# Banded attention into a gated conv feed-forward: another order table, with part of the output stores issued by GpSimd

## The chip, the cores and the metric

One core of a Trainium2 chip. The metric is the device time of one execution in microseconds; of several runs the median is given. PE is the TensorE matrix engine, DVE VectorE, ACT ScalarE, POOL GpSimd, and SP the queue engine that issues most transfers here.

## The reference

Inputs q, k, v are [8, 8, 576, 64] float32: 8 batches, 8 heads, 576 positions, head size 64. The feed-forward has w_in [512, 1024], conv_w [3, 1024] and w_out [1024, 512].

```python
scores = (q @ k.transpose) / 8
scores = where(|i - j| <= 32, scores, -1e9)
attn = softmax(scores) @ v
x = attn, heads side by side              # [8, 576, 512]
h = maximum(x @ w_in, 0)                  # [8, 576, 1024]
conv = sum over 3 taps k of conv_w[k] * h shifted by k - 1 positions
out = (h * sigmoid(conv)) @ w_out         # [8, 576, 512]
```

## The kernel before

The kernel first builds a list of operations (`Work.op`), each with a name, what it reads and writes, and the slots of buffers it takes. Nothing is issued then. Afterwards `Work.emit` walks through a text, `ORDER`, written out in full: each token is an operation's number, the letter of the engine that issues it (P for PE, V for DVE, S for ACT, G for POOL, D for a transfer on SP's queue) and the buffer indices it takes. `1F` lets PE do one idle matmul. All engines keep this order (`keep_in_program_order`), so the text fixes, for every engine, what runs after what, and which engine does each operation that several could do.

Attention, for each batch b: `load q/k b i` brings four heads of q or k into a slot of the pool `st` (0.59 MB each), `cast` makes bf16 from it into `qkb`, `tr` transposes on PE into PSUM, `ev` evicts into `qkT`. `sc` computes the scores of a half (x) of a head group in three PSUM banks, with only the 128 keys that a block of 64 queries can see; `exp` on ACT writes them to `attn`, `mask` multiplies by 0 and 1 (for batch 0, `sca` adds a large negative matrix on PE before the scores, and there is no mask). `load v b c` and `cast v b c` bring a 128-row piece of v with a border of 32 into `ve`; `vo hi` and `vo lo` copy its halves into `vo`, shifted by 64 rows. `av` multiplies, `rec` takes the reciprocal of the row sums, `mul` writes `xn`. A turn then makes `xT`: `xt` on PE and `ex` (kind e), or a transposing transfer `xd` (kind d), by the table `TURNS`.

The feed-forward works on chunks c = 0 to 11 of 384 positions, three for each pair of batches, and on eight blocks m of 128 of the 1024 columns. `ph` is four matmuls with `w_in_sb` (385 columns or so), `relu` writes `hT` (pools hT0, hT1, hT2 by the chunk's place in the pair). The convolution's three taps are shared out by a letter for each block in `CONV`: 3, 2 and 1 are the number of taps that PE does by diagonal matrices `diag_w` (`pc`), the rest on DVE (`tap`); q lets POOL multiply two taps (`cp`) and add them (`cs`) and DVE the third; r one tap on POOL, two on DVE; s two on POOL, one on PE, with a `sum` on DVE. `tanh` on ACT, `gate` on DVE to `gT`, then `py` multiplies by `w_out_sb`, `y` evicts 128 rows to a slot of the pool `y`, and `store c i` writes them out (0.26 MB). Chunk 1 is done in two halves (`SPLIT`).

w_in comes in three transfers (`load w_in 0, 1, 2`: columns 0 to 255, 256 to 511, 512 to 1023) and is cast block by block; w_out in two. The number of buffers of each pool is in `BUFS`.

The letters of the engines mean, in the two helpers that matter here:

```python
loader = {"D": sync, "Q": scalar}
...
loader[e_].dma_start(out_rows[r0:r0 + 128, :], y_sb.ap)
```

Of the kernel before, what the change touches and what calls it, by code (L numbers as in the profile page):

```python
# [40 lines left out]
class Work:  # L41
# [45 lines left out]
BUFS = {'st': 3, 'qkb': 6, 'qkT': 3, 'attn': 2, 'rec': 6, 'xn': 2, 'hT0': 7, 'hT1': 9, 'hT2': 9, 'cp': 6, 'gT': 3, 'y': 6}  # L87
TURNS = ('eeeee', 'eeede', 'eeeed', 'ddddd', 'ddddd', 'ddddd', 'ddddd', 'ddddd')
MASKS = ('aa', 'mm', 'mm', 'mm', 'mm', 'mm', 'mm', 'mm')
CONV = (  # L90
    'r2333q33',
    '221223s321s2213r',
    'r3q3332s',
    'r333s3q3',
    '22q33q33',
    'q32sqq2q',
    '33qq2rqq',
    '2q3q3qrr',
    'qqrqqq33',
    '32qrqqqr',  # L100
    'rqq2qq3q',
    '2r22qqrq',
)
ORDER = """
11D0 12D 13D1 14D 16D 18D 15D 22S0 0V 19D 20G1 41P010 23V 21G 42P 45P23 43S 46P 48S 44V 47V 17D 124D2 24S2 28G 125D
50P4560 52S 51S 25V 61P031 26V3 27S 1P1 2V 62P 64S 3V 126D0 65P25 66P 67S 33G 29V 35G 68V 56P413 63S 135D1 59S 53S
58S 70P2501 76P361 30G 36G 71S 31S 79S 73S 57S 4V 34V 77S 81P20 90P1 72S 78S 84P0 93P4 85V0 37V 91V1 82V2 38G 99P3
86V 92V 94V3 32S 100V4 40V 117P5 102P6 83V 103V5 104V 39G 8G 136D 140D 2F 130G 111P0 112V0 113V 108P1 109V1 110V
127G 128G 95S 88P2 118V2 97P6 89V 129G 101S 106P0 98V 115P1 131G 1F 141D 139D 137D2 132G 1F 107S 116S 250P4 294P2
138D 133V 119V 134V 240D0 251S00 10V 360P3 262G0 142D 145V4 144S5 295S1 361V2 272P6 273S3 7V 149S 263V0 264V 338P1  # L110
1F 339V4 161P542 162S 164P23 368G12 275P6 276V 270S 271V 165V 369G 163S 370G 5G 382P7 292S 293V 166S 155V 6G 122P1
316P5 317V5 296P0 371V2 167P4631 314S 146G1 171S 383S6 170S 169S 123V 380S 315V 150G 241D1 404P5 179P370 405S0 180V
381V 995D 340P6 358S 154G 173P410 318P5 176S 181V 359V 147G0 9G 406P3 438P2 244V 992D2 182P17 148G 336S 424S 337V
439S01 384P6 183S 245V 425V 243G 177S 151G 482P5 483V1 402S 526P2 504P1 403V 184S 185P3050 441P6 172V 158V 994D 153G
527S2 175S 178V 529P7 530V 159V 187S 188S 570P2 592P4 460P3 143D 461V3 593S4 548P0 546S 547V 996D 487P3 249G 189S
571S5 191P475 195S 242G 426P2 190V 194S 463P5 430P7 585G34 549V6 246V 197P01 488V 248S 464V 156G 442V 505S7 206P1
157G 247G 193S 196V 215P4 458S 427P 459V 507P6 480S 481V 428S0 200P5 216V5 431P 1001G2 198V0 508V 990D0 489V 586G
207V1 199S 991D 218P2 217V 209P0 201V3 997D 594P4 524S 208V 152G 998D 502S 503V 434P1 432S1 550P3 160G 525V 202V
219V4 210V2 211V 233P7 224P6 234V0 227P5 228V5 435P 225V1 235V 587G 204P0 226V 213P7 220S 222P6 568S 229V 993D 612S
436S2 205V 214S 1030P251 613V 238P1 658P0 724P7 1003G 223S 1032S 614P4 659S3 1031V 999G3 230D 1000G5 702P6 1091D1  # L120
1092D 615S1 569V 725V2 729P5 617P0 703S4 239S 673G50 768P2 769S5 730V 1012P432 1093D0 705P7 618V 1006G 731V 1004V
634S 1013S 1015P61 706V 744S 635V 1014S 1016S 636P2 745V 1005V 637V0 680P4 1007G 588P0 1094D 589V 1002G4 681V6 722S
723V 746P3 1033P65 747S1 1034V 1096D 1017S 802P2 1018P4731 641P6 676P1 1011V 674G 1035S 642V 590S 780G2 803S82 675G
677V 824P5 846P2 643V 1020S 1022S 790P4 678S 1021S 656S 825V2 1100G1 1101S0 591V 679V 657V 683P3 781V7 684V 1024P501
1027S 791P 1023V 847S0 814G1 748P6 1026S 792V3 1028S 766S 700S 1113P020 1114S 1116P54 782V 1009G 1115V 701V 815V1
1118S 767V 1095D 1097D 1102G2 1131P022 1132S 1133S 826P3 844S 1117V 854G43 855G 1029V 1036P4600 1038S 1040S 868P2
788S 890P5 794P4 1039S 437D 1758D2 856G 816V 857V0 789V 891S3 866S 429D 1103G3 1042P675 1106G 869V1 1010V 870P2 795P
1098D 867V 845V 822S 823V 1104V 1134P03 1045S 1099D 1105V 793D 1044S 1046S 1047V 1008G 1048P10 1057P7 1066P5 1049V3
1058V2 1756D1 796S4 934P6 1135S 912P4 1067V0 888S 1050V 1041G 1762D 1084P0 1069P1 889V 1075P2 1136S 956P3 935S7
892P6 1110G 1085V1 1076V4 1757D 1070V5 913S4 1071V 1051P4 1086V 1078P1 1060P0 1079V3 1759D 1059S 798P7 1767G5 1760D  # L130
1107S 1077S 937P2 957V6 914P3 1068V 799P 1111G 433D 971G05 972G 973G 1061V5 910S 911V 1062S 1064P5 932S 1052V1 1053V
1108S 800S5 1080V 938V 954S 1065V 1761D 1055P6 1073P0 1082P4 933V 955V 978P7 1074S 1765G4 1778P151 1766G1 1119P3201
1083S 974P4 1056V 1192P6 1763D 1779S 1857D0 1236P1 1122S 1112V 1214P2 1780V 1123S 1121S 1125P503 975V 976S 1193V20
1127S 982P6 1258P5 977V 983P 1109G 1215V4 1216P4 1129S 1124V 1204G2 1859D1 1768G0 1128S 1237S3 1205V2 1206V 1771S
1137P3010 979P 984V2 1259S0 1769G 1130G 1212S 1861D 1213V 1143P652 1234S 1235V 1770V 1141S 1139S 1149P41 1158P1
1176P3 1140S 980V0 1167P0 1772G 1177V2 1324P7 1168V4 1147S 1142V 1346P2 1146S 1145S 1775G 1238P5 1260P6 1325S6
1280P7 1860D 1159V0 1178V 1148V 1179P3 981D 1764D 1150V5 1151V 1152P4 1160S 1256S 1278S 1169V 1185P1 1776G 1332G13
1279V 1170P0 1347S1 1281S5 1171V1 1161P6 1180V3 1162V2 1181V 1333G 1087D 1302P2 1172S 1186V5 1303S2 1781P73 1782S
986P0 1334G 1298P2 1348P7 1163V 797D 1153V0 1154V 1295G45 1796P640 1257V 1296G 1297G 1783S 1187V 1335V5 1299V 1304P3
987P 1866G2 1344S 1366S 1862D 1368P1 1858D 1798V 1345V 1300S 1879P452 1797S 1182D 1301V 1868G3 1367V 1784P6271 1322S  # L140
1323V 988S3 1788S 985D 1799P30 1870V 1787S 1773G 1369P 1376P7 1880V 1088D 1800S 1881S 1790P243 1801V 1774D 1370V1
1802P5010 1377P 1869V4 1871G 1164D 1786S 1794S 1793S 1777V 1789V 1792S 1795V 1378S0 1897P631 1806S 1863D 1867G1
1372P4 1814P20 1823P7 1832P1 1804S 1841P5 1373P 1824V4 1872V 1898S 1155D 1864D 1833V3 1805S 2526D 1380P6 1834S 1825V
1374V4 1842V1 1808P017 1446P4 1843V 1873S 2522D2 1812S 2524D1 1424P5 1381S01 1402P7 1383P6 1811S 1810S 1815V2
1882P10 1816V 1173D 1512P2 1188D 1189D 1403S1 1405P7 2523D 1425V2 2529D 1899S 1807G 1813V 1817P5 1835P3 2525D 1447S3
1384V 1400S 1826P4 1865D 1883V 1406V 1468P1 1827V0 1836V5 1884S 1432G02 2531G5 1513S4 1490P0 1534P2 1828V 1448P4
1401V 1379D 1469V5 1470P6 1837S 1844P1 1422S 1433G 1875G 1818V3 1850P3 1434G 1535S6 1491V7 1829D 1423V 1819S 1466S
1467V 1900P20 2533G2 1488S 1901S 1845V4 1846V 1536P7 1568P5 1435V4 1569S52 1554S 1489V 1902S 1498G35 1851V1 1656P2
1444S 1514P1 1590P5 1612P6 1375D 2535G 1555V 2528D 1499G 1576G14 989D 1852V 1445V 1591S0 1500G 1885P0730 1887S
1634P4 801D 1577G 1613V2 1615P5 1657S8 1847D 1501V0 1889S 1616V 1592P6 1874G 1532S 1560P2 2532G0 1556P3 1533V 1510S  # L150
1838D 1511V 1578G 2534V3 1888S 1878D 1820D 1635S1 1890V 2537S 1876D 1891P107 1632S 1633V 1610S 1664G20 1611V 1894S
1557P 1561P 1903P4561 2527D 1579V0 1893S 1678P1 1853D 1895S 1562S2 1722P7 1896V 1558V0 1907S 1909P236 1588S 1589V
1905S 1906S 1915P01 1924P4 1679V3 1908V 1877G 1933P5 2536V 1934V2 1649G53 1650G 1651G 1913S 1652P1 1564P6 1723S4
1911S 1958P7 1912S 2623D0 1665G 1565P 1980P2 1666G 1653V 1916V0 1654S 1686G41 1925V5 1926S 1935V 1667V3 1914V 1918P4
1700P5 1959S40 1936P7 1655V 1687G 1676S 1927P1 2530D 1917V 2624D 1730G30 1731G 1981S0 1982P0 1919V3 1677V 1559D
1688G 2625D2 2024P2 1920S 1689V3 2626D 1566S4 1942P4 1928V4 1945P6 1854D 1937V1 1929V 1938V 1930D 2025V3 1951P1
1943V5 1952V2 1701S7 2540G 1567D 2000S 2539S 1698S 2538G 2543V 1944S 2001V 1946V0 2632G1 2002P7 2003S6 1921D 2032G52
1703P2 1960P5 2629D 1732G 2562P400 1947V 2564S 2033G 2544P762 1953V 1699V 2545S 2546V 1733V0 1704V 2068P1 2069S5
2046P3 2010G14 2011G 1744P7 2034G 2112P6 1978S 2541D 2563S 2047S1 1720S 1979V 1563D 2035V1 1742S 2012G 2049P4 1721V
# [36 lines left out]
def kernel(  # L196
# [40 lines left out]
    gpsimd, sync = InOrder(nc.gpsimd), InOrder(nc.sync)  # L237
# [9 lines left out]
    qkb = pool("qkb", [128, RP, 2, 64], BF16)  # L247
    qkT = pool("qkT", [128, 4, W], BF16)
# [466 lines left out]
    def project(c, i):  # L715
# [19 lines left out]
        def emit_st(e_):  # L735
            r0 = c * CH + 128 * i
            loader[e_].dma_start(out_rows[r0:r0 + 128, :], y_sb.ap)
# [113 lines left out]
```

## Time and profile before

| | |
|---|---|
| runs | 240.04, 242.59, 241.75 us; median 241.75 |
| the profiled execution | 240.04 us, of which the span in the profile is 238.3 |
| busy in the span | PE 206.2, DVE 213.1, ACT 181.2, POOL 189.0 us |
| mean granted clock of PE | 0.98 |
| transfers | 46.75 MB, nearly all on SP's queue |
| chain that ended last | DVE 43%, PE 26%, "issue" 11%, POOL 8%, ACT 6% |

Each profiled instruction belongs to a group named by its engine, the operation and its tiles (all have one line, since a helper records them): `pf` is PSUM, `cp` POOL's products, `gT` the gated block. A group's line gives the number, the busy time and the mean ns of one, then the idle time of the engine before them with what released it. Ends overlap the start of the next instruction on PE, DVE and ACT, so durations of rows add up to more than busy time.

### The profile page before, as it was taken

How to read it: one execution, taken by the hardware profiler on the slowest of the kernel's cores; microseconds unless marked ns; L12 is line 12 of the kernel's file. 1: busy time of each engine (PE TensorE's matmuls, PEld its weight loads, DVE VectorE, ACT ScalarE, POOL GpSimd, SP SyncE). 2: the span in 40 equal slices, each digit the busy share in tenths (PEclk: the TensorE clock that was granted, in tenths of full speed). 3: DMA queues.
4: the chain of work that ended last, by engine and by line, in shares of the span. 5: the costliest groups of instructions: out<-in, count | busy, mean ns of one | idle time of the engine just before them, and what ended most of it. 6: DMA issues, size and time to landing. Idle time of an engine off the chain costs nothing.

```text
span 238.3 us, 7024 instructions
## 1 busy us (share of the span) xinstructions
PE 206.2 (87%) x2615; PEld 118.8 (50%) x2637; DVE 213.1 (89%) x473; ACT 181.2 (76%) x456; POOL 189.0 (79%) x256
## 2 busy tenths in 40 slices
PE   0868987899899998999998889899899879998972
PEld 0545646467555645555654555454555435544420
DVE  6729999899998999997789999998998998999991
ACT  2894797689999878788979788796889856735651
POOL 7068699878798888945999999889769496999920
PEclk9995999999999999999999999999999999999997
DMA  6999999967999957989999969720247503421034
GB/s 224 298 254 373 274 350 298 268 172 232 301 288 352 222 191 211 234 186 254 296 261 149 356 181 189 170 54 3 87 95 143 200 30 101 105 79 53 0 133 177
DMA packets 68166, 46.75 MB, mean 196 GB/s; under 512 B 52172, under 2 KB 53220, under 8 KB 68132
## 3 DMA queue, kind: packets, MB, share of 16 engines
q1 hardware_dynamic: 68096, 46.30, 72.6%
q8 instruction: 20, 0.33, 0.6%
q14 instruction: 14, 0.11, 0.2%
q10 hardware_dynamic: 36, 0.01, 0.0%
HBM read 32.52 MB, written 9.44 MB: 176 GB/s over the span
## 4 chain that ended last, share of the span: by engine, by line
DVE 43%; PE 26%; issue 11%; POOL 8%; ACT 6%; DMA 3%; SPq 2%; DVEq 0%; POOLq 0%; ACTq 0%
PE pf L234 26%; DVE pf L234 13%; DVE gT L234 11%; DVE attn L234 4%; POOL cp L234 4%; DMA vst<-in_v_dram 3%; DVE hT L234 3%; DVE qkT L234 3%; ACT pf L234 2%; DVE vo L234 2%; POOL vo L234 2%; SPq L234 2%; DVE xn L234 2%; DVE y L234 2%; ACT attn L234 1%
## 5 line engine op out<-in xcount | busy, mean ns | idle before, releaser
L234 PE MATMUL pf<-xT,w_in_sb 128*128 128x385 bf16 (+2 forms) x416 | 73.6, 316 | 2.2 <-DVE hT L234 0.8
L234 POOL TENSOR_SCALAR cp<-hT,conv_w_sb 128x384 f32<-128x384 bf16 (+1 forms) x89 | 61.7, 703 | 16.1 <-ACT hT L234 9.4
L234 PE MATMUL pf<-w_out_sb,gT 128*128 128x512 bf16 x266 | 68.7, 380 | 4.8 <-DVE gT L234 3.2
L234 ACT ACTIVATE pf<-pf 128x384 f32<-128x384 f32 (+1 forms) x104 | 47.1, 469 | 26.3 <-DVE pf L234 24.7
L234 DVE SCALAR_TENSOR_TENSOR gT<-pf,hT 128x384 bf16<-128x384 f32 (+1 forms) x104 | 51.1, 515 | 2.2 <-ACT pf L234 1.3
L234 PEld LDWEIGHTS <-w_in_sb 128*128 128x128 bf16 x416 | 38.5, 98 | 26.3 <-issue 2.8
L234 ACT ACTIVATE attn<-pf 128x512 bf16<-128x512 f32 (+1 forms) x96 | 42.4, 510 | 3.2 <-PE pf L234 2.3
L234 DVE SCALAR_TENSOR_TENSOR pf<-hT,conv_w_sb,cp 128x384 f32<-128x384 bf16 (+1 forms) x46 | 40.4, 881 | 2.3 <-issue 0.7
L234 PEld LDWEIGHTS <-gT 128*128 128x128 bf16 x288 | 26.1, 98 | 32.4 <-DVE gT L234 6.1
L234 POOL TENSOR_TENSOR cp<-cp,cp 128x384 f32<-128x384 f32 (+1 forms) x38 | 40.1, 1061 | 1.9
L234 ACT ACTIVATE hT<-pf 128x385 bf16<-128x385 f32 (+2 forms) x73 | 34.2, 487 | 5.5 <-PE pf L234 5.0
L234 PE MATMUL pf<-hT,diag_w 128*128 128x384 bf16 (+1 forms) x138 | 28.4, 311 | 2.1 <-DVE hT L234 1.5
L234 POOL TENSOR_SCALAR qkb<-st 128x1152 bf16<-128x1152 f32 (+2 forms) x24 | 28.2, 1179 | 0.6 <-DMA st<-in_q_dram 0.3
L234 ACT COPY qkT<-pf 128x576 bf16<-128x576 bf16 x44 | 27.1, 658 | 1.8 <-DVE xn L234 1.0
L234 ACT ACTIVATE xn<-pf,rec 128x64 bf16<-128x64 f32 x88 | 20.3, 328 | 5.9 <-DVE rec L234 5.7
L234 DVE TENSOR_TENSOR attn<-attn,mask 128x1152 bf16<-128x1152 bf16 x23 | 24.5, 1069 | 0.1
L234 PE MATMUL pf<-ident,qkb 64*128 64x64 bf16 x576 | 15.7, 196 | 9.1 <-POOL qkb L234 5.9
L234 DVE SCALAR_TENSOR_TENSOR pf<-hT,conv_w_sb,pf 128x384 f32<-128x384 bf16 (+1 forms) x39 | 20.7, 542 | 1.7 <-PE pf L234 1.2
L234 POOL TENSOR_SCALAR vo<-ve 64x520 bf16<-64x520 bf16 (+1 forms) x20 | 19.6, 980 | 2.6 <-PE pf L234 0.8
L234 PEld LDWEIGHTS <-qkT 64*128 64x128 bf16 x576 | 13.0, 98 | 15.2 <-issue 13.8
L234 DVE TENSOR_TENSOR xn<-pf,rec 128x256 bf16<-128x256 f32 x50 | 19.8, 412 | 0.5
L234 PE MATMUL pf<-qkT 64*128 64x64 bf16 x576 | 16.1, 195 | 4.4 <-DVE gT L234 2.1
(54 smaller groups left out, 238.4 us busy)
## 6 DMA issues: line engine op xcount, KB each, us to landing
st<-in_q_dram SPq DMA_DIRECT2D x16, 576.0 KB, 5.7
st<-in_k_dram SPq DMA_DIRECT2D x16, 576.0 KB, 6.6
out_dram<-y SPq DMA_DIRECT2D x36, 256.0 KB, 2.6
vst<-in_v_dram SPq DMA_DIRECT2D x24, 256.0 KB, 5.9
vst<-in_v_dram SPq DMA_DIRECT2D x16, 192.0 KB, 5.1
st<-in_moe_w_out_dram SPq DMA_DIRECT2D x2, 1024.0 KB, 10.1
vo<-ve SPq DMA_DIRECT2D x9, 130.0 KB, 3.3
st<-in_moe_w_in_dram SPq DMA_DIRECT2D x2, 512.0 KB, 6.0
```

Of the source, the lines that this page charges most:

```text
L234: return lambda *args, **kwargs: fixed(do(*args, **kwargs))
```

## The change

The order table is another one from end to end, and with it the numbers of buffers, the engine that each operation is given, and the taps' letters. In the code one line is changed: a store whose letter is G is issued by GpSimd.

```diff
-BUFS = {'st': 3, 'qkb': 6, 'qkT': 3, 'attn': 2, 'rec': 6, 'xn': 2, 'hT0': 7, 'hT1': 9, 'hT2': 9, 'cp': 6, 'gT': 3, 'y': 6}
-TURNS = ('eeeee', 'eeede', 'eeeed', 'ddddd', ...
+BUFS = {'st': 4, 'qkb': 5, 'qkT': 3, 'attn': 2, 'rec': 7, 'xn': 2, 'hT0': 5, 'hT1': 8, 'hT2': 7, 'cp': 6, 'gT': 3, 'y': 5}
+TURNS = ('eeeee', 'deeee', 'eeeed', 'ddddd', ...
-    'r2333q33',  '221223s321s2213r', 'r3q3332s', 'r333s3q3', '22q33q33', 'q32sqq2q', ...
+    '32r233q3',  'q2233r3q322q3321', 's33r3333', '2233r233', '32q32323', 'q2qs23qq', ...
-11D0 12D 13D1 14D 16D 18D 15D 22S0 0V 19D 20G1 41P010 23V 21G 42P 45P23 43S 46P 48S 44V 47V 17D 124D2 24S2 28G 125D
+0V 11D0 13D1 12D 15D 124D2 14D 16D 19D 22S0 20V1 21G 18D 41P010 23S 42P 45P23 46P 28S 47V 48V 135D3 43S 17D 24G2
...
-            loader[e_].dma_start(out_rows[r0:r0 + 128, :], y_sb.ap)
+            (gpsimd if e_ == "G" else loader[e_]).dma_start(out_rows[r0:r0 + 128, :], y_sb.ap)
```

What the two tables give to the engines, where they differ (number of operations, old to new):

| operation | engines |
|---|---|
| store | SP 36 to 21, POOL 0 to 15 |
| mask | DVE 23 to 19, POOL 5 to 9 |
| `cp` products, `cs` additions | POOL 89 to 78, 38 to 32 |
| units with 3, 2, 1 taps on PE | 30 to 36, 20 to 20, 8 to 5 |
| first taps from a `q` or `r` unit | DVE 46 to 43 |
| `ev` | ACT 44 to 40, DVE 20 to 24 |
| `mul` | ACT 22 to 18, DVE 50 to 54 |
| cast v | POOL 19 to 24, ACT 11 to 10, DVE 10 to 6 |
| cast q and k | POOL 24 to 26, ACT 6 to 4, DVE 6 to 6 |
| cast w_in | POOL 6 to 5, ACT 0 to 3, DVE 2 to 0 |
| `vo` (half copies) | POOL 20 to 16, DVE 11 to 16, SP 9 to 8 |
| relu | ACT 73 to 76, DVE 31 to 28 |

The first loads on SP's queue, in order (w_in by part):

```
old: q 0 0, k 0 0, q 0 1, k 0 1, v 0 1, v 0 3, v 0 0, v 0 4, v 0 2, w_in 0, w_in 1, w_in 2, q 1 0
new: q 0 0, q 0 1, k 0 0, v 0 0, w_in 0, k 0 1, v 0 1, v 0 4, v 0 3, q 1 0, v 0 2, w_in 2, w_in 1
```

## The prediction

> **What bounds the kernel now.** I read the busy times first, then busy time by stage, then the opening microseconds instruction by instruction.
>
> ```profile
> PE 206.2 (87%) x2615; PEld 118.8 (50%) x2637; DVE 213.1 (89%) x473; ACT 181.2 (76%) x456; POOL 189.0 (79%) x256
> ...
> 0.00:23.80 23.80, 14.02 (x250) 9.68 (x251) 15.31 (x56) 14.80 (x33) 13.75 (x57) 0.86 0.92 287
> 23.80:60.00 36.20, 32.60 (x488) 21.38 (x492) 33.98 (x88) 29.65 (x76) 30.60 (x44) 0.99 0.97 268
> 60.00:120.00 60.00, 56.59 (x858) 33.29 (x864) 55.25 (x129) 52.37 (x137) 48.92 (x47) 1.00 0.97 252
> 120.00:180.00 60.00, 54.45 (x658) 30.38 (x662) 57.02 (x111) 49.62 (x129) 54.17 (x61) 1.00 0.68 155
> 180.00:238.30 58.30, 48.57 (x367) 24.03 (x371) 51.58 (x93) 34.79 (x86) 41.51 (x50) 0.98 0.33 100
> ```
>
> The columns after the stretch are PE, PEld, DVE, ACT and POOL. From 23.8 us on, DVE is busy 197.8 of 214.5 us (92%) and PE 192.2 (90%), POOL next. No single wait ends that part. Before 23.8 us no engine reaches two thirds: the opening waits for transfers.
>
> ```profile
> 6.28 0.62 ACT L234 CAST qkb<-st 128x512 bf16<-128x512 f32 x1 [3.52 <-DMA st<-in_k_dram]
> ...
> 10.21 0.43 DVE L234 CAST qkb<-st 128x512 bf16<-128x512 f32 x1 [1.14 <-DMA st<-in_k_dram]
> ...
> 13.66 0.62 POOL L234 TENSOR_SCALAR ve<-vst 128x512 bf16<-128x512 f32 x1 [7.47 <-DMA vst<-in_v_dram]
> ...
> 15.78 0.62 POOL L234 TENSOR_SCALAR ve<-vst 128x512 bf16<-128x512 f32 x1
> ...
> 22.17 1.20 POOL L234 TENSOR_SCALAR w_in_sb<-st 128x512 bf16<-128x512 f32 x2 [0.22 <-DMA st<-in_moe_w_in_dram]
> ...
> 23.82 3.60 PE L234 MATMUL pf<-xT,w_in_sb 128*128 128x385 bf16 x20 [0.32 <-ACT xT L234]
> ```
>
> These are start, duration, instruction, and the wait before it. They give landings in queue order: the first k half at 6.28 us, the second at 10.21, the last of five v pieces just before 15.78, w_in at 22.17. The first feed-forward matmul starts at 23.82.
>
> **Part 1, the opening loads: +4.1 us.** The old order was q0, k0, q1, k1, five v pieces, then w_in. The new one is q0, q1, k0, v 0, w_in part 0, k1, v 1, v 4, v 3, batch 1's q0, v 2, and w_in parts 2 and 1. Pace from the rows above: a q or k half (0.59 MB) takes (10.21 - 4.88)/3 = 1.78 us, q0 having landed at 4.88; a v piece takes (15.78 - 10.21)/5 = 1.1; w_in (2.1 MB) takes 6.4, so its first quarter takes 1.6. That puts k0 at 8.4 us, k1 at 12.8 (2.6 late), v 2 at 19.0 (3.2 late), all of w_in at 23.8.
>
> The chain behind k1 in the new table: DVE casts it, but halfway comes `cast v 0 1`, which needs a piece landing at 13.95; the last cast ends at 14.9. After `conv_ev` and one `vo`, three evictions of 0.75 us stand on DVE before the scores: 17.7. Scores of the second head group to 19.2, six exponentials on ACT to 21.5 (old: 14.96 + 2.40 = 17.36). Then eight `av` at 0.45 us on PE: 25.1; DVE's reciprocal and four `mul` of 0.42 queued behind: 27.0; transpose 0.35, eviction 0.6. The first `ph` starts at 27.95 instead of 23.82. On POOL, `cast v 0 2` waits for v 2, with `vo hi 0 0 1`, `vo hi 0 1 2` and the first w_in cast queued behind it; they end by 22.7, inside that chain. A later `cast w_in 3` waits till 23.8, also covered. Low end of this term: 1.3 us, the 3.2 of v 2 less 1.9 that PE loses today in waits for `vo`. High end: 5, if those waits come back.
>
> **Part 2, work moved between engines.** I count each table and price by row:
>
> ```profile
> L234 DVE TENSOR_TENSOR attn<-attn,mask 128x1152 bf16<-128x1152 bf16 x23 | 24.5, 1069 | 0.1
> ...
> L234 POOL TENSOR_TENSOR attn<-attn,mask 128x1152 bf16<-128x1152 bf16 x5 | 12.4, 2482 | 8.4 <-ACT attn L234 8.4
> ```
>
> The last figure before the second bar is ns of one: a mask moved to POOL costs 2.48 for 1.07. Four are moved.
>
> DVE: masks -4.3, four first taps of `q` units (0.88 each, and fewer of them at half width) -3.7, v casts -4 x 0.58 = -2.3, three relus -1.4, two w_in casts, a diagonal and a y -2.2, q and k casts and sums -1.0; added: 4 `ev` +3.0, 4 `mul` +1.7, 5 `vo` +3.3, one more `r` unit +1.5. Total -5.4. The durations of all rows sum to 237.6 where the page has 213.1 busy, since ends overlap the next start, so this is worth -4.9.
>
> PE: six more three-tap units and three fewer one-tap units, 15 diagonal matmuls more: at 28.4 us for 138 it is +3.1, and as PE's rows sum to 243.3 for 206.2 busy, +2.7. ACT: -4.1, not at the limit. POOL: eleven products fewer (mostly at 0.71) -8.1, six additions (1.09) -7.0, masks +9.9, casts of q, k and v +6.1, `vo` -4.5, a diagonal more and a w_in cast less +0.6; net -3.0, without stores.
>
> **Part 3, 15 of 36 stores on POOL.** What they leave behind is not on the path: SP already stands idle waiting for results, and after the opening no engine shows a wait for a load.
>
> ```profile
> SPq L234 <- ACT y L234: 32.1, 8, 12.0
> ...
> L234 SPq DMA_DIRECT2D out_dram<-y x36: 332/438/3545, 61.6 to 234.4; - x36
> ```
>
> (The waits of SP's queue; then min, median and max ns of a store's issue.) So no gain from SP. POOL's own price isn't in this trace. From below: SP's median, 0.44 us, 6.6 for 15. From above: POOL's longest row, 2.48, 37 for 15. The only row of a compute engine's queue issuing a transfer is ACT's, 0.65 us; I take that, 9.8 us. Against total work it puts POOL at 195.8. Fourteen of the 15 stand 18 or more operations behind their `y` in the table, so POOL rarely waits for data; where it does, the products behind it are late next, then DVE's taps. At the very end two POOL stores (10 0 and 11 2) follow each other: +0.5 us, between 0 and 2.
>
> The Trainium skill (page "SBUF — State Buffer", sections "SBUF: two separate sides" and "A bandwidth-pool intuition that's wrong") speaks against this part: a transfer issued by GpSimd has its descriptors written through a port pair that certain DVE instructions lock, about 0.62 us alone and 3.1 beside a DVE copy. By those figures 15 stores would cost between 9.3 and 46 us of POOL, as an estimate; the low figure agrees with the 9.8 taken from the row and leaves the sum as it is, the high one would make POOL the bound. A row here that fits a shared port is the DVE tap that reads two SBUF operands, 882 ns, beside 614 where one comes from PSUM; no run here shows a store on POOL.
>
> **The body's sum.** Busy work after the first `ph`, old to new: DVE 202.0 to 195.2, PE 194.6 to 197.1, POOL 177.9 to 185.9. If only the largest total counts, 202.0 becomes 197.1: -4.9. But an engine can run ahead only as far as buffers allow, and the new table is uneven: cut into stretches of two chunks (from one chunk's first `ph` to that of the second after it), adding the busiest engine of each, it gives 206.4 old, 206.1 new; in stretches of one chunk 211.2 and 215.9, because POOL leads in several (its masks and casts come in lumps). gT has three buffers, hT fewer than before (5, 8, 7 for 7, 9, 9), so I take the two-chunk sum, -0.3, with -4.9 and +4.7 as ends.
>
> Sum: +4.1 - 0.3 + 0.5 = +4.3 us, a span of 242.6. The profiled execution took 240.04 for its span of 238.3, so 244.3; it was the fastest of three, and on the median of 241.75 it would be 246.0. I say 245.2, between the two.
>
> **Rivals.**
> (a) DVE's relief decides (faster). The place is 23.8 to 220 us, the price -4.9, and the opening costs only its low end 1.3, no tail: -3.6, about 237.3. For it: DVE is the busiest engine now, and `gT` and `hT` waits are the largest ones of PE. Against: PE gets 2.7 us more. It decides where the opening costs less than 2.4.
> (b) Both happen: +4.1 + 0.5 - 4.9 = -0.3, about 240.6: no change. For it: the totals are only two engines' averages apart; against: the one-chunk sums.
> (c) POOL becomes the bound. At 1.25 us a store (what SP's transposes take, 1.23) the one-chunk sum is 220.1, +8.9; with the opening and a tail of 1 it is +14, about 255; at 2.48 by two chunks, +7.1 and a tail of 2, +13. For it: POOL leads in the uneven stretches. Against: the old POOL shows 16 us of idle before products.
>
> **How the numbers follow.** Forecast 0.42, with its own range 242.5 to 250; (a) 0.24; (b) 0.19; (c) 0.15. A measurement of this kernel tells about 1% from no change, 239.3 to 244.2. Faster is (a), 0.24; the same is (b), 0.19; slower is the forecast and (c), 0.57. The range leaves out (a)'s lowest part and (c)'s highest: 236.8 to 253.
>
> **What would show it.** Opening: the first matmul from `xT` near 28 us, POOL's `ve` cast waiting till 19 us. Body: DVE busy near 208, PE 209, POOL 196 with stores of about 0.65 us. Tail: last y to the end some 0.5 us longer than today's 3.9. I am wrong if the first `ph` starts before 25.5 us, or if DVE's share rises with PE's in the body.

## The result and the profile after

The changed kernel takes 250.94 us (median of four runs, 250.09 to 252.0) where the kernel before takes 241.53 beside it: a ratio of 1.040, with an interval of 1.032 to 1.047. It is 9.4 us slower. I had said 245.2, 3.5 us more: the direction was right, the size was not. The profiled execution took 252.0 us for a span of 250.3.

Busy times of the changed kernel:

```profile
PE 208.9 (83%) x2627; PEld 121.2 (48%) x2652; DVE 219.9 (88%) x463; ACT 176.3 (70%) x440; POOL 190.7 (76%) x258
```

PE went from 206.2 to 208.9, as worked out. DVE was to fall to 208 and rose to 219.9, with ten instructions fewer. That line points at the step that failed.

The same work by stages, cut at the first feed-forward matmul and at the first relu of chunks 2, 4 and 8. First the changed kernel, then the kernel before with its own moments (columns PE, PEld, DVE, ACT, POOL, then the granted clock):

```profile
0.00:27.38 27.38, 14.55 (x251) 10.14 (x252) 16.60 (x57) 13.79 (x32) 13.51 (x53) 1.00 1.03 289
27.38:66.50 39.12, 33.83 (x488) 22.68 (x491) 36.14 (x82) 28.15 (x74) 32.86 (x47) 0.91 0.85 244
66.50:124.30 57.80, 49.18 (x752) 28.08 (x760) 52.08 (x101) 43.53 (x113) 44.44 (x42) 0.97 0.95 227
124.30:182.00 57.70, 53.06 (x675) 29.70 (x682) 55.68 (x112) 44.81 (x105) 50.24 (x55) 1.00 0.65 168
182.00:250.30 68.30, 58.30 (x482) 30.55 (x481) 59.37 (x114) 45.97 (x118) 49.60 (x63) 0.99 0.30 94
```

```profile
0.00:23.82 23.82, 14.02 (x250) 9.70 (x251) 15.34 (x56) 14.80 (x33) 13.75 (x57) 0.86 0.92 287
23.82:59.30 35.48, 31.90 (x483) 20.85 (x486) 33.26 (x88) 28.95 (x74) 29.98 (x43) 0.99 0.97 265
59.30:110.10 50.80, 47.38 (x742) 27.90 (x746) 48.08 (x109) 44.54 (x116) 41.15 (x39) 1.00 0.94 250
110.10:168.30 58.20, 53.41 (x655) 29.89 (x661) 54.26 (x105) 47.67 (x120) 54.10 (x59) 1.00 0.81 183
168.30:238.30 70.00, 59.51 (x493) 30.42 (x498) 62.21 (x119) 45.27 (x117) 49.97 (x61) 0.98 0.34 103
```

The differences are +3.6, +3.6, +7.0, -0.5 and -1.7 us, 12.0 in all: this profile is of the slowest of four runs, that of before of the fastest, so they differ by more than the medians' 9.4. All that is lost is lost by chunk 4; the second half gives 2.2 back. In the third stretch DVE does eight instructions fewer and is busy 4.0 us longer.

Over the whole kernel it shows in these groups. The first line is of the kernel before, the others are of the changed one:

```profile
L234 DVE COPY vo<-ve 64x1040 bf16<-64x1040 bf16 x5 | 3.6, 718 | 0.3 <-POOL ve L234 0.2
...
L233 DVE TENSOR_TENSOR attn<-attn,mask 128x1152 bf16<-128x1152 bf16 x19 | 22.5, 1183 | 0.2 <-ACT attn L233 0.2
L233 DVE COPY vo<-ve 64x1040 bf16<-64x1040 bf16 x9 | 10.2, 1139 | 0.3
L233 POOL TENSOR_TENSOR attn<-attn,mask 128x1152 bf16<-128x1152 bf16 x9 | 22.1, 2451 | 4.2 <-ACT attn L233 4.0
L233 POOL DMA_DIRECT2D out_dram<-y x15 | 8.9, 593 | 4.8 <-ACT y L233 4.8
```

A mask on DVE was 1069 ns and is 1183; the wide copy to `vo` was 718 and is 1139. The same instruction with the same shape takes longer, so something seems to hold it. Single instructions show what; this is the timeline of the changed kernel at two of the places:

```profile
47.85 2.36 POOL L233 TENSOR_TENSOR attn<-attn,mask 128x1152 bf16<-128x1152 bf16 x1
...
48.09 2.27 DVE L233 COPY vo<-ve 64x520 bf16<-64x520 bf16 x1
...
50.26 0.22 PE L233 MATMUL pf<-ve,attn 128*64 128x65 bf16 x1 [1.07 <-POOL attn L233]
...
51.77 0.21 PE L233 MATMUL pf<-ve,attn 128*64 128x65 bf16 x1 [1.22 <-DVE gT L233]
...
98.45 2.74 POOL L233 TENSOR_TENSOR attn<-attn,mask 128x1152 bf16<-128x1152 bf16 x1
...
99.01 2.48 DVE L233 COPY vo<-ve 64x1040 bf16<-64x1040 bf16 x1
...
102.13 1.12 PE L233 MATMUL pf<-hT,diag_w 128*128 128x384 bf16 x3 [2.42 <-DVE gT L233]
```

The narrow copy takes 290 ns at its fastest, the wide one 425. Here they take 2270 and 2480: both end within 0.3 us of POOL's mask. `gate 3 1` stands behind the second in DVE's queue, and PE waits 2.42 us for it. That the wait is put down to DVE hides the culprit: it is on another engine. (The wait of 1.07 us at 50.26 is of another kind: there PE needs the result of POOL's mask itself.)

I went through all nine POOL masks of the changed kernel in the trace. Each has a DVE instruction beside it that reads SBUF alone (a copy, a cast, a mask, or a tap with `hT` and `cp`) and ends as POOL's mask does or shortly behind it:

| mask on POOL, start us | held on DVE | ns | ns alone |
|---|---|---|---|
| 1 1 1, 47.8 | `vo hi 1 3 4` | 2265 | 290 |
| 2 1 1, 80.0 | `mask 2 1 0` | 2368 | 745 |
| 3 1 0, 98.4 | `vo hi 4 0 2` | 2475 | 425 |
| 4 0 0, 115.3 | `cast v 5 2` | 2011 | 420 |
| 4 1 0, 119.1 | `vo lo 4 2 4` | 2478 | 425 |
| 5 1 0, 144.9 | `mask 5 1 1` | 2381 | 745 |
| 6 0 0, 171.9 | `mask 6 0 1` | 2970 | 745 |
| 6 1 0, 176.9 | `vo hi 7 2 4` | 1492 | 425 |
| 7 0 1, 201.2 | `tap 8 4 2 1` | 1936 | 605 |

The differences add up to 15.6 us. In the kernel before, five masks hold four such instructions, for 4.5 us (2772 for 745, 1958 for 605, and two casts of 1079 and 894 for 420). The 11.1 us between them are nearly the 11.7 by which DVE's 219.9 misses my 208.2, but masks are not all that holds. Counted for every DVE instruction of the table that reads SBUF alone and has POOL at work beside it, against the fastest of its shape in all these runs, held time is 26 us in the kernel before and 35 in the changed one: 9 us more, since the changed kernel has fewer additions on POOL, which held DVE too. DVE's instructions that read PSUM are not held: beside the same masks an `xn` product keeps its 423 ns and an eviction of `y` its 680. In the profiles of the two kernels none of the 679 that read PSUM, and none of the 39 that read SBUF alone while POOL stands idle, takes more than 0.05 us above the fastest of its shape.

### The profile page after: what moved, and what is told of

Read it like the earlier page. It is cut to its first block, busy times and chain, and to the rows that moved or that the text cites. A ratio compares the mean times of both kernels' runs of the same rounds, so it can differ in the third digit from the quotient of the medians.

```text
span 250.3 us, 7023 instructions
## 1 busy us (share of the span) xinstructions
PE 208.9 (83%) x2627; PEld 121.2 (48%) x2652; DVE 219.9 (88%) x463; ACT 176.3 (70%) x440; POOL 190.7 (76%) x258
## 4 chain that ended last, share of the span: by engine, by line
DVE 40%; PE 32%; issue 12%; POOL 5%; ACT 4%; DMA 4%; SPq 1%; POOLq 0%; DVEq 0%; ACTq 0%
PE pf L233 32%; DVE pf L233 12%; DVE gT L233 9%; DVE vo L233 4%; DMA st<-in_k_dram 4%; DVE attn L233 4%; POOL cp L233 3%; ACT attn L233 2%; DVE xn L233 2%; DVE hT L233 2%; DVE qkT L233 2%; DVE ve L233 1%; DVE rec L233 1%; SPq L233 1%; POOL vo L233 1%
## 5 line engine op out<-in xcount | busy, mean ns | idle before, releaser
L233 POOL TENSOR_SCALAR cp<-hT,conv_w_sb 128x384 f32<-128x384 bf16 (+1 forms) x78 | 53.7, 697 | 24.0 <-ACT hT L233 15.2
L233 DVE SCALAR_TENSOR_TENSOR pf<-hT,conv_w_sb,cp 128x384 f32<-128x384 bf16 (+1 forms) x43 | 37.8, 890 | 1.7 <-POOL cp L233 0.6
L233 PE MATMUL pf<-hT,diag_w 128*128 128x384 bf16 (+1 forms) x153 | 32.5, 316 | 4.2 <-DVE gT L233 4.0
L233 POOL TENSOR_SCALAR qkb<-st 128x1152 bf16<-128x1152 f32 (+2 forms) x26 | 30.2, 1166 | 6.6 <-PE pf L233 3.8
L233 POOL TENSOR_TENSOR cp<-cp,cp 128x384 f32<-128x384 f32 (+1 forms) x32 | 33.7, 1056 | 1.2
L233 ACT COPY qkT<-pf 128x576 bf16<-128x576 bf16 x40 | 24.5, 657 | 2.8 <-PE pf L233 2.6
L233 POOL TENSOR_TENSOR attn<-attn,mask 128x1152 bf16<-128x1152 bf16 x9 | 22.1, 2451 | 4.2 <-ACT attn L233 4.0
L233 DVE COPY qkT<-pf 128x576 bf16<-128x576 bf16 x24 | 17.4, 747 | 6.0 <-PE pf L233 5.4
L233 DVE TENSOR_TENSOR attn<-attn,mask 128x1152 bf16<-128x1152 bf16 x19 | 22.5, 1183 | 0.2 <-ACT attn L233 0.2
L233 PE MATMUL pf<-ve,attn 128*64 128x65 bf16 x320 | 16.8, 207 | 6.1 <-DVE y L233 1.5
```

What stands on the lines that cost most here:

```text
L233: return lambda *args, **kwargs: fixed(do(*args, **kwargs))
```

## Experiments

Each run is the changed kernel (or, from its name with b, the kernel before) with the edit named; e6 builds on e5, e7 to e9 on e6. Times are medians, ratios are to the kernel before, which took 240.7 to 241.2 us beside them. Two theories stood first: held copies, and POOL as the bound.

**e1, the held copies on ScalarE.**

```diff
-159V  1774V 1872V 1777V 1875V 2643V     vo hi 1 3 4, vo hi 4 0 2, cast v 5 2, vo lo 4 2 4, vo hi 5 0 2, vo hi 7 2 4
+159S  1774S 1872S 1777S 1875S 2643S
```

> The changed kernel with six copies of DVE (five vo copies and one v cast, those that took 1.3 to 2.5 us beside a POOL instruction where the fastest of their kind take 0.4) done by ACT at the same places of the table. Theory of the blocked copies: the six lost 9.6 us on DVE, and two of them (at 48 and 99 us) stopped PE and were followed by 10.2 us at a granted clock of 0.5. Expected 243 to 246 us against 250.9, with the low clock in mid-kernel gone. Theory of the uneven table: POOL and PE lead in turns whatever these copies do; expected 249.5 to 251.

Measured: 247.94, ratio 1.027 (1.023 to 1.032), between the two theories' ranges; DVE 219.9 to 210.5. So 3.0 us come from there. Half clock did not go altogether: 3.4 us of it are left, behind 51.3. Of the five masks that had held one of these copies four now hold nothing. Beside the first the next instruction in DVE's queue was held in the copy's stead: `tap 1 0 0 1` (192 columns) took 2.25 us at 48.05. The mask, not the copy, is the thing to move.

**e2, the old order of the first 13 loads.**

```diff
-load q 0 0, q 0 1, k 0 0, v 0 0, w_in 0, k 0 1, v 0 1, v 0 4, v 0 3, q 1 0, v 0 2, w_in 2, w_in 1
+load q 0 0, k 0 0, q 0 1, k 0 1, v 0 1, v 0 3, v 0 0, v 0 4, v 0 2, w_in 0, w_in 1, w_in 2, q 1 0
```

> The changed kernel with the first thirteen loads in the order of the kernel before, all else as it is. If the opening is a term of its own, the first ph starts near 24 us instead of 27.4 and the time falls by 3 to 3.6, to 247.5. If the blocked copies and the clock after them swallow what is gained (they stand at fixed places of the table), less than 1 us is left.

Measured: 253.04, ratio 1.051 (1.046 to 1.056), 2 us worse, and the first `ph` at 30.36. The table's engines were not changed with the loads: ACT has `cast v 0 0` ahead of the evictions, and this piece now came late (a wait of 6.6 us). The run says only that load order and engine order belong together; e6 does it again with both.

**e3, all 36 stores on SP.**

```diff
-store 0 0 G, 0 2 G, 0 1 G, 1 0 G, ... (15 stores)
+store 0 0 D, 0 2 D, 0 1 D, 1 0 D, ...
```

> The changed kernel with all 36 stores on SP's queue at the same places of the table. The 15 stores took POOL 8.9 us, 0.59 each. Theory of the blocked copies: POOL is not the bound, so 250 to 251.5. If POOL's own work sets the pace, 244 to 248.

Measured: 252.22, ratio 1.048 (1.043 to 1.052), POOL 182.5 us busy. Taking 8 us off POOL gains nothing: neither POOL's amount of work nor its stores bound the changed kernel. I had expected 251.5 at most.

**e4, idle matmuls where PE stops.** Behind the changed kernel's stops at 50 and 100 us the granted clock is 0.50, for 6.8 and 3.4 us. 41 small matmuls on zeros at the stops keep PE busy:

```diff
+12Z5 (behind py 0 0), 9Z5 (behind av 1 1 0), 20Z4 (behind av 3 0 2)
```

> The changed kernel with 41 small matmuls on zeros (240 columns, into unused columns of PSUM) put on PE where it stood still at 48 to 52 and 99 to 102 us; the copies stay blocked as they are. If the half clock after these stops costs PE time, the granted clock stays at 1.0 there and 2 to 4 us are gained (half of 10.2 us at most): 247 to 249. If the clock is only a mark of idleness and costs nothing, 251 to 252.

Measured: 250.95, ratio 1.042 (1.038 to 1.045). The clock was full from 29.6 to 248.1 us, and the time stayed. The half clock goes with the loss; by this run it is not its cause.

**e5, the nine masks on DVE.**

```diff
-mask 1 1 1 G, 2 1 1 G, 3 1 0 G, 4 0 0 G, 4 1 0 G, 5 1 0 G, 6 0 0 G, 6 1 0 G, 7 0 1 G
+mask 1 1 1 V, 2 1 1 V, 3 1 0 V, 4 0 0 V, 4 1 0 V, 5 1 0 V, 6 0 0 V, 6 1 0 V, 7 0 1 V
```

> The changed kernel with its nine GpSimd masks given to VectorE, all else as it is. Theory (a GpSimd mask holds the next VectorE instruction that has SBUF operands only until it ends; in the changed kernel's trace nine masks hold copies, masks and taps for about 15.0 us beyond their own durations): VectorE loses the 15.0 us and gets 9 x 0.76 = 6.8 us of masks, busy 219.9 to about 212, GpSimd 190.7 to about 168.5, no copy of v above 0.8 us, and the median falls to 243 to 247. Rival 1 (VectorE is the limit by its amount of work, masks on GpSimd relieve it by 0.76 us each): 254 to 257. Rival 2 (the new table's uneven order and its fewer buffers lose the time, whoever masks): 249 to 251.5.

Measured: 247.92, ratio 1.027 (1.020 to 1.033), 0.9 above what I gave the theory and 1.1 below rival 2. What decides is DVE: nine instructions more, and it is busy 7 us less, 212.9, as the theory had it. Of these 7 us 3.0 reach the end. About 1.1 of the 3.0 may be another gain of the same move: PE no longer waits for the result of a POOL mask, as it did at 50.26.

```profile
L231 DVE TENSOR_TENSOR attn<-attn,mask 128x1152 bf16<-128x1152 bf16 x28 | 26.4, 952 | 0.2 <-ACT attn L231 0.2
...
L231 DVE COPY vo<-ve 64x1040 bf16<-64x1040 bf16 x9 | 6.2, 691 | 0.3
```

The copies fell from 1139 to 691 ns. The masks' mean of 952 is not 745, and one copy still took 1.38 us: casts and sums on POOL hold DVE too.

**e6, masks on DVE and an opening whose loads and casts fit.**

```diff
 loads: q 0 0, k 0 0, q 0 1, k 0 1, v 0 1, v 0 3, v 0 0, v 0 4, v 0 2, w_in 0, w_in 2, w_in 1, q 1 0
 cast v 0 0 moved behind exp 0 0 1 2; cast v 0 1 and load v 1 1 behind cast k 0 1 4 9
```

> As the run before it, and the first loads in the order q0, k0, q1, k1, v pieces, w_in, with the casts of v 0 and v 1 moved behind the casts of k and the first exponentials, so that no engine stands waiting for a piece that comes late. Theory (the opening's 3.6 us pass on to the end): the first feed-forward matmul comes at 24 to 25.5 us instead of 27.4, and the median is 2.5 to 3.5 below the run with the masks alone, 240 to 244. Rival (the body has slack that takes up a late start): the first matmul comes as early, but the median is within 1 us of the run with the masks alone.

Measured: 245.60, ratio 1.018 (1.012 to 1.024), 2.3 us below e5. The first `ph` came at 25.69 for e5's 27.49, a little later than expected. 1.8 us earlier there, 2.3 less at the end: the opening passes on. The runs of the two overlap (246.18 to 248.55 and 244.02 to 247.09), so the 2.3 is a rough figure; in the profiles the lead is 2.7 us at the first relu of chunk 3 and 2.9 at the end. PE's longest wait behind the opening stood at one place, here on DVE and on PE:

```profile
79.57 3.05 DVE L231 TENSOR_TENSOR attn<-attn,mask 128x1152 bf16<-128x1152 bf16 x1
...
82.68 0.22 PE L231 MATMUL pf<-ve,attn 128*64 128x65 bf16 x1 [2.75 <-DVE attn L231]
```

`mask 2 1 1`, now on DVE, was held by two POOL casts of q (79.74 to 82.0).

**b_masks_on_pool: the suspected cost put into the kernel before.** Of its own five POOL masks four go to DVE (4 1 0 is on POOL in both kernels), and the other eight of the changed kernel's nine come to POOL.

> The kernel before with the nine masks on GpSimd that the changed kernel has there, in place of its own five; nothing else is changed. Theory (each such mask costs VectorE the time for which it holds the next instruction, about 1.67 us, and saves only 0.76): VectorE busy +2 to +5 us in spite of four masks less, median 243 to 247. Rival (masks are priced by their rows, so VectorE is relieved by 4 x 0.76 = 3 us): 238 to 241.

Measured: 263.61, ratio 1.089 (1.081 to 1.098). DVE's 216.2 us (+3.1) is what the theory said, the time is far above both. A wait of PE and POOL's row show a second price that I had left out, that of the queue:

```profile
PE pf L232 <- POOL vo L232: 8.6, 4, 3.1
```

```profile
L232 POOL TENSOR_TENSOR attn<-attn,mask 128x1152 bf16<-128x1152 bf16 x9 | 21.9, 2429 | 18.4 <-ACT attn L232 18.3
```

In the old table these masks wait 18.3 us on POOL for their exponentials, and the copies to `vo` queued behind them are late for PE (8.6 us, 1.1 before). So this run is no clean measure of the holding. It shows that a mask's place in POOL's queue can cost more than its duration.

**b_stores_on_pool: only the 15 stores, in the kernel before.**

```diff
-loader[e_].dma_start(out_rows[r0:r0 + 128, :], y_sb.ap)
+(gpsimd if e_ == "G" else loader[e_]).dma_start(out_rows[r0:r0 + 128, :], y_sb.ap)     with 15 letters D to G
```

> The kernel before with the same 15 stores issued by GpSimd as in the changed kernel, at their places in the old table; nothing else is changed. Theory (a store takes 0.6 us of an engine that has that much idle time): GpSimd busy +8 to +10 us, median 240 to 243. Rival (stores on GpSimd hold the products queued behind them, or are held by VectorE's copies): 245 to 252, with single stores above 1.5 us.

Measured: 248.66, ratio 1.031 (1.027 to 1.035): the rival's time, by neither of its reasons in full. No store took over 0.73 us, and POOL's waits for data grew little:

```profile
L232 POOL DMA_DIRECT2D out_dram<-y x15 | 8.9, 594 | 6.9 <-ACT y L232 6.9
```

(5.1 of the 6.9 stand at the end, before the last store, and hold nothing.) Against the first profile, 1.6 us had been lost by the first relu of chunk 1, before any store (see b_same). And DVE was held longer, 3.8 us in all over the same instructions: `tap 2 0 2 1` took 1958 ns for 752, beside a sum, `store 0 0` and a cast in a row; `tap 9 6 2 1` took 2547 for 611 beside four products and a sum. So stores lengthened POOL's unbroken rows there. How the 7.4 us divide is not settled.

**e7, e8: one mask earlier in DVE's order.**

```diff
-tap 2 3 2 1, ev k 3 1 0, mask 2 1 1
+mask 2 1 1, tap 2 3 2 1, ev k 3 1 0
```

> The run with the masks on VectorE and the earlier loads, and one mask more moved within VectorE's order: mask 2 1 1 stands before the tap of unit 2 3, so that it starts near 78 us and not at 79.6, where two casts of q on GpSimd held it for 3.05 us while TensorE waited 2.8 us for it. Theory (held instructions set the pace wherever the scores or the gate need them): the mask takes 0.75 to 1.2 us, the first relu of chunk 3 comes 2 to 3 us earlier (91.8 to about 89), median 242.5 to 244.5 for 245.6. Rival (another instruction of VectorE is held by the same casts instead, or the stage is limited by amounts of work): median within 1 us of 245.6.

Measured: six runs at 239.09, 240.39, 245.78, 247.22, 247.31 and 248.85; median 246.5, as the rival had it. But that is not a spread around one time, it is two times. The profile fell on a quick one (span 238.5), so I took two more of the same kernel:

> The kernel of the last run of the changed table once more, unchanged, for another profile. If it takes 246 us or more: theory (TensorE stops at one place for about 2.5 us or more because a mask or a gate is held on VectorE, and runs at half clock for 3.4 or 6.8 us behind it): one or two such stretches, at 48 to 58 or 80 to 90 us, where the profile at 240.4 us has none. Rival (a late landing in the opening): all of the loss stands before the first relu of chunk 1, and the clock is full.

> The same kernel a third time, with the same expectation: half clock behind a stop of TensorE if it takes 246 us or more, none if it takes 239 to 241.

They took 244.24 and 246.52. Up to the first relu of chunk 2 (63.5, 63.2, 64.0 us) and from chunk 3 to the end the three agree within 0.8 us. Between the two relus they take 24.3, 27.9 and 29.4. The last, at 246.52, has half clock at 48.3 to 51.7 and at 85.8 to 89.2, as the theory had it for so slow a run. But the one at 244.24 loses 3.6 us between the same relus at full clock throughout, so a slow time does not need half clock. The rival, a loss in the opening, fell. The timelines show where it is. This is the quick run, then the first of the two others (DVE's lines above POOL's in each):

```profile
79.03 0.62 DVE L231 SCALAR_TENSOR_TENSOR pf<-hT,conv_w_sb,cp 128x384 f32<-128x384 bf16 x1
...
78.45 0.59 POOL L231 DMA_DIRECT2D out_dram<-y  x1
79.08 1.04 POOL L231 TENSOR_SCALAR ve<-vst 128x512 bf16<-128x512 f32 x1
80.25 2.27 POOL L231 TENSOR_SCALAR qkb<-st 128x1152 bf16<-128x1152 f32 x2
```

```profile
79.61 3.32 DVE L231 SCALAR_TENSOR_TENSOR pf<-hT,conv_w_sb,cp 128x384 f32<-128x384 bf16 x1
...
79.04 0.59 POOL L231 DMA_DIRECT2D out_dram<-y  x1
79.66 0.63 POOL L231 TENSOR_SCALAR ve<-vst 128x512 bf16<-128x512 f32 x1
80.24 2.27 POOL L231 TENSOR_SCALAR qkb<-st 128x1152 bf16<-128x1152 f32 x2
```

In both the tap's row starts 0.05 us ahead of POOL's cast. In the one it keeps its 0.62 us and the cast takes 1.04 for 0.63. In the other the cast keeps its 0.63, and the tap stands through it and the two casts that follow without a gap, 3.32 us. The third profile is like the second: the tap starts 0.05 us ahead and takes 3.32. Between the two relus DVE's instructions that read SBUF alone are held for 2.7 us in the quick run and for 6.3 and 6.8 in the others, so what is lost there, 3.6 and 5.1 us, is in the main held time. In these three profiles a near tie goes with the two times of the whole kernel.

**e9, the tap out of the way.**

```diff
-tap 2 3 2 1, ev k 3 1 0, mul 2 0 1, tap 2 3 2 2, ..., mul 2 1 3
+ev k 3 1 0, mul 2 0 1, ..., mul 2 1 3, tap 2 3 2 1, tap 2 3 2 2
```

> The changed kernel with masks on VectorE, earlier loads and mask 2 1 1 early, as before, and the two taps of unit 2 3 moved in VectorE's order from before the eviction ev k 3 1 0 to behind mul 2 1 3, when GpSimd's three casts are over. Nothing is added or taken away. Theory (a tap that starts just after one of the casts is held for all three, 3.3 us): the slower times of 244 to 249 us go, all runs lie within 238 to 241.5, the tap takes 0.6 to 0.9 us. Rival (the slower times come from another place, or another instruction is held in the tap's stead): runs still spread over 239 to 248.

Measured: median 243.5 of twelve runs, 240.32 to 246.15; ratio 1.006 (1.002 to 1.009) by the nine runs below 244. Better than e6, but not the narrow band that I expected: the tap still met the second cast of q and took 1.56 us. It is a step, not the cure.

**b_fewer_held and b_five_moved: the same for the kernel before.**

```diff
-mask 6 0 1 G, mask 7 1 0 G, vo lo 6 2 4 V
+mask 6 0 1 V, mask 7 1 0 V, vo lo 6 2 4 S          (b_five_moved also: mask 2 1 0 V, vo lo 2 2 4 S)
```

> The kernel before with its two GpSimd masks that hold a VectorE instruction (6 0 1 and 7 1 0) given to VectorE, and its one copy of v that was held for 0.9 us (vo lo 6 2 4) to ScalarE. Theory (held time is a price of its own): VectorE loses about 3.1 us held by the masks and 1.35 for the copy and gets 1.5 of masks, busy 213.1 to about 210, median 238 to 240.5. Rival (these places have slack, TensorE is as full as VectorE there): 240.5 to 243.

> The kernel before with the three moves that made it 1% faster (masks 6 0 1 and 7 1 0 to VectorE, vo lo 6 2 4 to ScalarE), and two more: mask 2 1 0, which in one profile held a tap for 2.78 us and in another did not, to VectorE, and vo lo 2 2 4, held for 0.9 to 1.3 us, to ScalarE. Theory: the spread of the kernel before goes, all runs within 1.5 us, median 237 to 239. Rival (mask 2 1 0 on VectorE costs its 0.75 us there and ScalarE's copy delays an eviction): 239 to 241.

Measured: three moves 238.90, ratio 0.990 (0.985 to 0.994), DVE 209.4 us busy: faster than both kernels, as the theory said. Five moves 240.49, ratio 0.997 (0.995 to 1.000): no better than three and above the 237 to 239 expected, though its twelve runs lie within 2.4 us where 23 of the kernel before lie within 5.0. The fourth and fifth move were not worth making. Its runs had a granted clock of either 0.973 to 0.979 or 0.998 to 1.000, with mean times of 240.7 and 240.0 us. Whether the lower clock costs these 0.7 us or only goes with a stop, this does not show.

**b_same, the kernel before once more.**

> The kernel before once more, unchanged, for a second profile. Theory (the opening of the first profile was no typical one: in two other runs of the old table the last needed piece of v landed 1.4 to 1.8 us later, though nothing ahead of it was changed): span 239 to 241, the cast of v 0 2 at 16.5 to 17.6 us instead of 15.8, the first feed-forward matmul at 25 to 25.6. Rival (the delays came from the edits): 15.8 and 23.8 again.

Measured: span 242.3 in a run of 244.0, above what the theory had. The first `ph` came at 24.37 for 23.82, between what the two theories said, so the opening varies by some 0.5 us here and by 1.8 in b_stores_on_pool (25.60). Much of the rest is again a hold. These are DVE's and POOL's lines of this profile, then the same tap in the first one:

```profile
71.47 2.78 DVE L232 SCALAR_TENSOR_TENSOR pf<-hT,conv_w_sb,cp 128x384 f32<-128x384 bf16 x1
...
71.47 2.36 POOL L232 TENSOR_TENSOR attn<-attn,mask 128x1152 bf16<-128x1152 bf16 x1 [1.05 <-ACT attn L232]
```

```profile
68.79 0.61 DVE L234 SCALAR_TENSOR_TENSOR pf<-hT,conv_w_sb,cp 128x384 f32<-128x384 bf16 x1
```

In the profile that I predicted from, `tap 2 2 2 1` had ended 1.0 us before `mask 2 1 0` began. Held time as counted above is 4 us more here than there, and the span is 4.0 us longer. Two of 23 runs of the kernel before exceed 243 us. In the changed kernel's profile all nine masks meet an instruction that they hold.

## Why the prediction was right and wrong

- **Opening, +4.1 us: right.** k0 was cast at 9.21 us (said 8.4), k1 at 13.27 (12.8), `cast v 0 2` on POOL at 19.82 (19.0), the first `ph` started at 27.38 (27.95): +3.6, or +3.0 against the second profile of before. (POOL stood before that cast for ACT's `cast v 0 3`, 2.25 us, and not for the piece itself, as I had it. By its own terms k1 is due at 12.9, not 12.8.) These are the loads of the changed kernel as its casts saw them:

```profile
9.21 1.24 ACT L233 CAST qkb<-st 128x512 bf16<-128x512 f32 x2 [6.44 <-DMA st<-in_k_dram]
...
13.27 0.83 DVE L233 CAST qkb<-st 128x512 bf16<-128x512 f32 x2 [0.86 <-DMA st<-in_k_dram]
...
27.38 1.48 PE L233 MATMUL pf<-xT,w_in_sb 128*128 128x385 bf16 x8
```

- **Work moved, DVE -4.9 us: the step that failed.** I multiplied counts by mean durations. "A mask moved to POOL costs 2.48 for 1.07" priced POOL's side and DVE's saving, and put at nothing that 2.48 us on POOL can stand in DVE's way. DVE measured +6.8: beside the nine masks its instructions lost 15.6 us, beside the old five 4.5. The trace that I predicted from had the sign of it: masks on DVE took from 743 to 2772 ns there, and the 882 ns that I gave for a tap with two SBUF operands is a mean from 589 to 1958. PE was right (+2.7 for +2.7, though 3.1 scaled as I scaled it is 2.6); POOL came out at 190.7 for 196.
- **Stores, 0.65 us each on POOL: the price was right** (0.593; 8.9 us in all for 9.8), and SP off the path: right (e3). That they cost the kernel nothing beyond the tail holds in the changed table (e3); in the old one the same stores cost 7.4 us (b_stores_on_pool), for which my sum had no term. The Trainium skill (page "SBUF — State Buffer", "A bandwidth-pool intuition that's wrong") has 0.62 us alone and 3.1 beside a DVE copy for a transfer that GpSimd issues. No store of the changed kernel, of b_stores_on_pool or of e6 took more than 0.73 us of POOL, so the second figure was not met here. The same page ("SBUF: two separate sides") has the port pair that DVE and GpSimd share as an exclusive lock, kept by the first to start for one whole instruction. I weighed it for the stores and should have weighed it for masks and copies, where the table of nine agrees with it. For the tap that stood through three casts one instruction is too short.
- **Tail, +0.5 us: right.** From the end of the last `y` (245.74) to the end of the span it is 4.6 us for 3.9.
- **Body, -0.3 us between -4.9 and +4.7: wrong, +8.4.** From the first `ph` to the end, 214.5 us became 222.9. My 202.0 for the old DVE lay 4.2 above the 197.8 that the profile has there. The ends came from sums of the same durations, so they could not hold a cost that depends on what meets what. My test for it, DVE's share rising with PE's, did not fit either: from the first `ph` on PE's share fell from 90% to 87% (194.4 of 222.9 us), and DVE's went from 92% to 91%, with more held time in it.
- **Rivals.** (c), with 255, was nearest in size, by the wrong engine: POOL is not the bound (e3). (a) and (b) needed DVE's relief, which was not there. That the kernel got slower, as I said, I owe to the opening's term; the body, the larger part of the loss, I had at about nothing.

By the runs, the 9.8 us from 241.1 to 250.94 go like this: masks on DVE take away 3.0 (250.94 to 247.92), the fitting opening 2.3 (245.60), one mask and one tap out of POOL's way 2.1 (243.5). The 2.4 that are left are not assigned by a run. In e9's profile the first `ph` still comes at 25.47 us (23.82 and 24.37 in the two of before) and the tail is 0.3 us longer, which would be 1.4 to 1.9 of them if it passes on whole; and e9 still has held instructions. e1 took 3.0 by another way, of the same holds. The fewer buffers were not tried alone, but e7 has them, with the changed letters, and its quick runs took 239.09 and 240.39: they need not cost anything.

## What to carry to other kernels

Don't price a move by the mean of a row alone: look at the spread of the row, and where an instruction takes three times its fastest, look at what another engine does in the same microseconds. Long instructions on POOL, and unbroken rows of short ones, are a cost to DVE's copies, casts, masks and taps that read SBUF alone; put them where DVE has instructions that read PSUM, or give them to DVE. The kernel before has such a place: beside its `mask 4 1 0` on POOL, at 108.5 us, DVE has reciprocals, products and an eviction of `y`, all from PSUM, and none is held. When one kernel runs at two times, compare two profiles of it at the stretch where they part, before explaining either.

## What the runs showed of the hardware that I had not expected

- Of two instructions whose rows start 0.05 us apart, in the same order each time, now DVE's got through first (once) and now POOL's (twice). The loser can wait for several instructions: a tap of 0.62 us took 3.32 beside three POOL casts of 0.63, 1.16 and 1.15 us.
- Behind stops of PE such as the 2.42 us before 102.13 the granted clock was 0.50 for 3.4 or 6.8 us; preventing all 10.2 us of it (e4) left the median where it was, 250.95 for 250.94.
- A store of 0.26 MB issued by POOL landed in 2.8 us by the median, 2.6 by SP; in b_stores_on_pool it was 3.8 and 2.6.
